# A hand-ordered attention and snake-MLP kernel: the steps of its first three blocks in another order

## The chip, the core and the metric

The kernel runs on one core of a Trainium2 chip. The metric is the time of one execution on the device in microseconds (us). It was measured three times before the change: 296.65 us is the median, 296.1 and 298.42 us are the lowest and highest. All rows of a profile come from one more execution, which the hardware profiler recorded.

## What is computed

For 8 batches, 8 heads, 576 positions and a head size of 64 the reference forms decayed causal attention without a softmax, lays the heads side by side, and sends the 4608 rows through a two-layer network of width 2048 whose activation is h + sin²(αh)/α:

```python
scores = scale * np.matmul(q, k.transpose(0, 1, 3, 2))
Dmat = np.where(rel >= 0, gamma[:, None, None] ** rel, 0.0)   # rel = row - column
x = np.matmul(scores * Dmat, v)          # heads side by side: (4608, 512)
h = x @ w_in                             # (512, 2048)
g = h + np.sin(alpha * h) ** 2 / (alpha + 1e-09)
out = g @ w_out                          # (2048, 512), float32
```

## The kernel before

**Blocks.** The first 512 positions of each batch make one block of 512 rows (blocks 0 to 7); the last 64 positions of all eight batches make block 8. For each block the attention gives x, transposed, as an fp16 tile xT; 16 projections of 128 channels follow (four products of 128x128 by 512 columns each), then sine, square and product for each channel group, and the second matrix product.

**Engines.** TensorE (PE) does all products. ScalarE (ACT) does every sine. VectorE (DVE) does every product step (square times 1/α plus h, read from PSUM), and the masks. Squares, casts of the loaded fp32 data to fp16, and evictions of PSUM go to ACT, DVE or GpSimd (POOL) as each step says. SyncE (SP) issues the loads of q, k and v, the transposing DMAs and the stores; POOL issues the eight loads of 512 KB of the weights.

**The steps, with their lines.** `load(b, nm, p)` (L147) brings half p of q, k or v of batch b into one of six buffers raw0 to raw5. `cast` (L171, the work in L207 or L122) makes fp16 of it. For batches 0 and 1 PE transposes (`turn`, L234, work in L240) and `take` (L247, work in L120 and L122) copies to kT or qT; from batch 2 on `crossed` (L226, L230) does it by a DMA. Within a batch `outer` (L312, L325) forms sums of k times v, `take_sum` and `evict` bring them to the tile kvs, `next_sum` (L352), `more` (L367, two instructions L370 and L371, on POOL) and `to_state` (L358; L361 on ACT, L363 elsewhere) chain them over the four chunks of 128 rows; `scores` (L379, L389), `masked` (L397, L401), `values` (L409, L430) and `add_states` (L441, L451) make the block's output and `keep` (L458) copies it to xT. `project` (L560, L568), `sine` (L573, L576), `square` (L581, L585 on ACT, L587 elsewhere) and `product` (L590, L592) work on one channel group; `gemm2(n, u)` (L600, L605) multiplies a quarter of the 2048 channels (part u mod 4) into the output rows of chunk u div 4; `finish` (L594) copies that bank to fp32 and stores it. `keep_busy(n, tag, m)` (L727, L730) issues n products of zeros of m columns; nothing reads them. `wait_for_w_in(g)` and `wait_for_w_out(g)` (L736, L740) are small DMAs from a weight tile, which hold SP's queue until that weight has landed.

**What sets the order.** L784 to L1263 are a list of these steps, written out, for blocks 0 to 2 (and what batches 3 and 4 need early). Each engine runs its instructions in the order of the list; between engines semaphores keep the dependencies. The number of the buffer that a step takes is read from the table BUFFERS (L19), in the order of the list; PSUM banks (h0, h1, h2, op of one bank, m0 and m1 of two) stand in the steps. From L1265 on a loop over n = 3 to 8 makes the order of the other blocks; there a block's second product is done in seven products of quarters (L671) in place of `gemm2` from n = 4 on.

The piece of the list that matters most for batch 1 (L937 to L970, with steps left out):

```python
        load(1, "v", 0)
        cast(1, "v", 0, G_)
...
        load(1, "k", 1)
        cast(1, "k", 1, G_)
...
        load(1, "v", 1)
        cast(1, "v", 1, A_)
...
        gemm2(0, 15, "h2")
        at[1].outer((1,), "h0", "h1")
        at[1].take_sum(2, A_)
```

Of the kernel before, what the change touches and what calls it, by code (L numbers as in the profile page):

```python
# [19 lines left out]
    "raw": "012345012345012345102405314023140240124012401240",  # L20
    "k16": "0123012302131313",
    "q16": "0120120121202020",
    "v16": "0123012310230123",
    "kT": "0123012310232323",
    "qT": "0123013210232323",
    "kvs": "00000000",
    "s16": "01010101",
    "xT": "01202020",
    "s32": "010101010101010101010",
    "ret": "01230123012313020213021302130213",  # L30
    "s": "012312013021302130210213021302130231032032103102320132013201320132013201320132013201320132013201320132013201320132013201320132013201320132013201",
    "ss": "012302130123012032103213021302103210321031203120312031203120312031203120312031203120312031203120312031203120312031203120312031203120312031203120",
# [4 lines left out]
def kernel(  # L37
# [74 lines left out]
    def load_w_out(g):  # L112
        nc.gpsimd.dma_start(w_out16[:, 4 * g : 4 * g + 4, :], w_out_r[:, g])
# [169 lines left out]
    class Attention:  # L283
# [268 lines left out]
    ops = {}  # L552
    PART = {None: slice(0, 512), 0: slice(0, 256), 1: slice(256, 512)}
# [46 lines left out]
    def gemm2(n, u, tag, cols=slice(0, 512)):  # L600
        c, part = divmod(u, 4)
        if (n, c, cols.start) not in ops:
            ops[n, c, cols.start] = psum.tile([P, 512], F32, tag=tag, bufs=1, name="ops")
        for fk in range(4 * part, 4 * part + 4):
            matmul(  # L605
                ops[n, c, cols.start][:, cols], gT[n][:, fk, c * P : (c + 1) * P], w_out16[:, fk, cols],
                start=(fk == 0), stop=(fk == FC - 1), skip_group_check=True,
# [173 lines left out]
    with tc.manual_schedule():  # L781
# [9 lines left out]

        keep_busy(7, "op", 128)
        keep_busy(6, "h0", 256)
        keep_busy(11, "op", 128)
        load(0, "k", 0)
        load(0, "q", 0)
        load(0, "v", 0)
        cast(0, "k", 0, V, (0,))
        cast(0, "k", 0, G_, (1,))
        turn(0, "k", 0, "op")  # L800
        cast(0, "q", 0, V, (1,))
        cast(0, "q", 0, V, (0,))
        turn(0, "q", 0, "h0")
        load(0, "k", 1)
        cast(0, "k", 1, G_, (0,))
        invert_alpha()
        cast(0, "v", 0, A_)
        at[0].outer((0,), "h1", "h2")
        keep_busy(8, "op", 256)
# [645 lines left out]
```

## Time and profile before

| what | value |
|---|---|
| median of three runs | 296.65 us (296.1 to 298.42) |
| the profiled execution | 298.54 us; its span from first to last instruction is 296.8 us |
| PE, DVE, ACT, POOL busy in the span | 284.6, 227.5, 207.3, 136.0 us |
| mean granted TensorE clock | 0.994 |
| first projection of block 0 starts | 21.16 us |
| projection 0 of block 3, the first step of the loop, done | 108.65 us |
| bytes moved by DMA | 50.08 MB, 169 GB/s |

Busy shares alone do not tell what a change can win: an engine that is busy 96% of the span may lose its other 4% in one place. So the profile is read by stages of the span, and in each stage by the wait that ends last. In a row of the timeline the columns are start, duration, engine, line, operation, tiles written and read, shape, count; square brackets give the idle time before it and what ended it. A row that joins several matmuls ends when the last one has drained: one of 512 columns is shown with 379 ns, but in the row of 24 of them from 77.98 us the starts are 216 ns apart ((5.35 - 0.379) / 23 us).

### The profile page before, as it was taken

The page shows a single profiled execution, that of the slowest core. Times are in us where ns is not written, and L with a number is a line of the kernel's source. Part 1 is how long each engine was busy: PE and PEld are TensorE (multiplying, and loading weights), DVE is VectorE, ACT ScalarE, POOL GpSimd, SP SyncE. Part 2 cuts the span into 40 slices and gives each one's busy share as a digit, 9 for nine tenths or more (in the row PEclk, how much of TensorE's full clock was granted, in tenths as well). Part 3 has the DMA queues.
Part 4 walks back from the last instruction along what each step waited for, and adds up shares of the span by engine and source line. Part 5 has one row for each costly group of instructions (what it writes and reads, how often), then busy time and mean ns, then how long its engine had stood idle before and what let it go on. Part 6 is the DMA issues. An engine that isn't in the chain of part 4 may idle for free. (4 is left out here: it accounts for less than half of the span.)

```text
span 296.8 us, 8464 instructions
## 1 busy us (share of the span) xinstructions
PE 284.6 (96%) x3480; PEld 183.6 (62%) x3480; DVE 227.5 (77%) x336; ACT 207.3 (70%) x341; POOL 136.0 (46%) x151
## 2 busy tenths in 40 slices
PE   6789997999999999999999999999999999999994
PEld 4666544555554554455767766776667676777783
DVE  2597873897628979778977598759876987987884
ACT  2579924798776796788866996698669657865510
POOL 5684676448299687652197219901970000000000
PEclk9999997999999999999999999999999999999999
DMA  7999999999899698967876897789962102111213
GB/s 218 347 232 210 247 255 286 281 257 242 220 204 218 102 185 175 270 162 143 156 200 202 147 189 183 220 145 157 222 163 58 40 10 81 35 38 35 71 33 111
DMA packets 122918, 50.08 MB, mean 169 GB/s; under 512 B 79872, under 2 KB 120832, under 8 KB 122880
## 3 DMA queue, kind: packets, MB, share of 16 engines
q1 hardware_dynamic: 118928, 44.78, 62.7%
q0 software_dynamic: 2688, 4.19, 7.8%
q10 hardware_dynamic: 1264, 0.58, 0.8%
q8 instruction: 27, 0.44, 0.6%
q14 instruction: 11, 0.09, 0.1%
HBM read 36.75 MB, written 9.44 MB: 156 GB/s over the span
## 5 line engine op out<-in xcount | busy, mean ns | idle before, releaser
L592 DVE SCALAR_TENSOR_TENSOR gT<-ss,inva,hps 128x512 f16<-128x512 f16 x144 | 105.4, 744 | 29.2 <-ACT ss L585 25.3
L576 ACT ACTIVATE s<-hps,alpha_t 128x512 f16<-128x512 f32 x144 | 96.8, 682 | 44.3 <-PE hps L568 43.9
L568 PE MATMUL hps<-xT,w_in 128*128 128x512 f16 (+1 forms) x532 | 121.3, 372 | 0.7 <-DMA w_in<-in_moe_w_in_dram 0.3
L568 PEld LDWEIGHTS <-w_in 128*128 128x128 f16 x596 | 66.6, 114 | 50.7 <-issue 1.4
L585 ACT ACTIVATE ss<-s 128x512 f16<-128x512 f16 x107 | 67.3, 630 | 2.8
L605 PE MATMUL ops<-w_out,gT 128*128 128x512 f16 x192 | 47.6, 385 | 0.0
L671 PEld LDWEIGHTS <-gT 128*128 128x128 f16 x384 | 37.5, 98 | 8.3
L207 POOL TENSOR_TENSOR k<-raw,cn 128x1024 f16<-128x1024 f32 (+1 forms) x17 | 28.9, 1703 | 7.5 <-DMA raw<-in_k_dram 7.5
L671 PEld LDWEIGHTS <-S 128*128 128x128 f16 x288 | 27.7, 98 | 5.3
L605 PEld LDWEIGHTS <-gT 128*128 128x128 f16 x192 | 18.1, 99 | 20.8 <-issue 0.6
L363 POOL TENSOR_TENSOR s<-kvs,cn 128x256 f16<-128x256 f32 x17 | 10.4, 612 | 41.8 <-DVE S L652 25.4
L207 POOL TENSOR_TENSOR q<-raw,cn 128x1024 f16<-128x1024 f32 x13 | 24.6, 1903 | 4.5 <-DMA raw<-in_q_dram 4.3
L671 PE MATMUL hps<-T,gT 128*128 128x256 f16 x192 | 22.9, 273 | 0.0
L671 PE MATMUL hps<-w_out,gT 128*128 128x256 f16 x192 | 22.9, 273 | 0.0
L671 PE MATMUL hps<-w_out,S 128*128 128x256 f16 x192 | 22.8, 273 | 0.0
L401 DVE TENSOR_TENSOR ret<-sc,mask 128x1024 f16<-128x1024 f32 x16 | 19.2, 1219 | 1.6 <-PE sc L389 1.4
L371 POOL TENSOR_TENSOR kvs<-s,kvs 128x256 f32<-128x256 f32 x21 | 16.0, 762 | 5.5 <-ACT kvs L120 2.8
L120 ACT CAST xT<-o 128x1024 f16<-128x1024 f32 (+1 forms) x15 | 16.5, 1129 | 2.7 <-PE o L451 2.7
L587 DVE TENSOR_TENSOR ss<-s 128x512 f16<-128x512 f16 x29 | 14.3, 495 | 3.0 <-ACT s L576 2.8
L370 POOL TENSOR_TENSOR s<-kvs,cn 128x256 f32<-128x256 f32 x21 | 13.3, 635 | 6.4 <-ACT kvs L120 6.3
L717 DVE TENSOR_TENSOR osb<-hps,low 128x512 f32<-128x512 f32 x13 | 9.0, 692 | 9.2 <-PE hps L671 9.2
L652 DVE TENSOR_TENSOR S<-gT,S 128x1024 f16<-128x1024 f16 x24 | 15.5, 685 | 0.0
(83 smaller groups left out, 274.6 us busy)
## 6 DMA issues: line engine op xcount, KB each, us to landing
raw<-in_q_dram SPq DMA_DIRECT2D x16, 512.0 KB, 5.4
out_dram<-osb SPq DMA_DIRECT2D x32, 256.0 KB, 2.8
raw<-in_k_dram SPq DMA_DIRECT2D x8, 512.0 KB, 6.1
raw<-in_v_dram SPq DMA_DIRECT2D x8, 512.0 KB, 5.3
raw<-in_v_dram SPq DMA_DIRECT2D x32, 128.0 KB, 3.4
raw<-in_k_dram SPq DMA_DIRECT2D x32, 128.0 KB, 3.2
w_in<-in_moe_w_in_dram POOLq DMA_DIRECT2D x4, 512.0 KB, 11.8
w_out<-in_moe_w_out_dram POOLq DMA_DIRECT2D x4, 512.0 KB, 13.1
```

The source lines that it names most:

```text
L120: eng.copy(d_, s_)
L207: eng.tensor_tensor(dst[:, a0:a1].rearrange("p a r t d -> p t (a r) d"), t_.rearrange("p (t a) x -> p t a x", t=2)[:, :, a0:a1].rearrange( ...
L371: nc.gpsimd.tensor_tensor(self.kvs[:, c], s32, self.kvs[:, c], ADD)
L401: nc.vector.tensor_tensor(ret.rearrange("p t (z x) -> p (t z) x", z=2)[:, :, 0:n], sc.rearrange("p t (z x) -> p (t z) x", z=2)[:, :, 0:n], ...
L568: matmul(hps_of[n, fc][0][:, cols], w_in16[fc // 4][:, a, fc % 4 :: 4], xs[n][:, a, cols], start=(a == 0 and part != 1), stop=(a == KT - 1 ...
L576: nc.scalar.activation(s_t, hps, mybir.ActivationFunctionType.Sin, bias=0.0, scale=alpha_t[:, fc : fc + 1],)
L585: nc.scalar.activation(ss_t, s_t, mybir.ActivationFunctionType.Square)
L587: eng.tensor_tensor(ss_t, s_t, s_t, MULT)
L592: nc.vector.scalar_tensor_tensor(gT[n][:, fc, :], ss_t, inva[:, fc : fc + 1], hps, MULT, ADD)
L605: matmul(ops[n, c, cols.start][:, cols], gT[n][:, fk, c * P : (c + 1) * P], w_out16[:, fk, cols], start=(fk == 0), stop=(fk == FC - 1), sk ...
L652: return eng.tensor_tensor(out_, x, y, op)
L671: matmul(acc[:, 256 * j : 256 * j + 256], lhs[:, x, 128 * j : 128 * j + 128], rhs[:, x], start=(tag is not None and j == js[0] and p == 0 ...
```

## The change

It leaves the loop from n = 3 on as it was and writes the list for blocks 0 to 2 anew: nearly every step stands elsewhere. The arithmetic is the same, with these differences:

- The tables of buffers are other ones for these blocks. In particular `load(1, "v", 1)` now takes raw2, the buffer of `load(1, "v", 0)`, where it had raw5 and the other raw3.
- Order of the first loads: q, k, v, q, k, v of batch 0 in place of k, q, v, k, q, v.
- Products of zeros: 50 in place of 36, all after the first transposes: 1 of 512 columns, 26 of 74, 20 of 128, then single ones; before, 24 of them stood ahead of the first real product.
- Steps on other engines: over the whole program squares on ACT, DVE and POOL are 97, 37 and 10 (before 107, 29 and 8); casts of v on ACT 12 (6), states on ACT 28 + 4 instructions (24); one `more` is on DVE; several casts and takes are halved between engines.
- Which of a chunk's four quarters comes first in `gemm2` is free: it is known from a list of the parts done.
- 14 instructions more run on PE, all of them zero products. The bytes moved and the waits for weight tiles are as many as before.

```diff
 BUFFERS = {
-    "raw": "012345012345012345102405314023140240124012401240",
+    "raw": "051243520202405124145312054231401240124012401240",
...
-        def more(self, c):
+        def more(self, c, eng=nc.gpsimd):
 
             s32 = place("s32", [P, 4, D], F32)
-            nc.gpsimd.tensor_tensor(s32, self.kvs[:, c - 1], g1.unsqueeze(2).to_broadcast([P, 4, D]), MULT)
-            nc.gpsimd.tensor_tensor(self.kvs[:, c], s32, self.kvs[:, c], ADD)
+            eng.tensor_tensor(s32, self.kvs[:, c - 1], g1.unsqueeze(2).to_broadcast([P, 4, D]), MULT)
+            eng.tensor_tensor(self.kvs[:, c], s32, self.kvs[:, c], ADD)
...
+        done = parts_of.setdefault((n, c), [])
+        done.append(part)
         for fk in range(4 * part, 4 * part + 4):
             matmul(
                 ops[n, c, cols.start][:, cols], gT[n][:, fk, c * P : (c + 1) * P], w_out16[:, fk, cols],
-                start=(fk == 0), stop=(fk == FC - 1), skip_group_check=True,
+                start=(len(done) == 1 and fk == 4 * part), stop=(len(done) == 4 and fk == 4 * part + 3),
+                skip_group_check=True,
             )
```

The new list at the start (`G_`, `V`, `A_` are POOL, DVE, ACT; steps of one engine after another are joined in a line):

```python
        load(0, "q", 0); load(0, "k", 0); load(0, "v", 0); load(0, "q", 1); load(0, "k", 1)
        cast(0, "k", 1, G_)
        cast(0, "q", 0, V, (0,)); cast(0, "q", 0, V, (1,))
        cast(0, "k", 0, V, (1,)); cast(0, "k", 0, V, (0,))
        turn(0, "q", 0, "h1"); keep_busy(1, "op"); turn(0, "k", 0, "h2"); keep_busy(26, "op", 74)
        cast(0, "q", 1, V)
        load(0, "v", 1); load(1, "q", 1); load(1, "q", 0); load(1, "k", 0)
        take(0, "q", 0, V); cast(0, "v", 0, A_); load_w_in(0)
        take(0, "k", 0, A_, (0,)); take(0, "k", 0, A_, (1,)); keep_busy(20, "h0", 128)
        turn(0, "q", 1, "op"); at[0].scores(0, 1, "m0")
        take(0, "q", 1, A_, (0,)); take(0, "q", 1, V, (1,))
        at[0].outer((0,), "op", "h0"); at[0].scores(0, 0, "m1"); at[0].take_sum(0, A_); load_w_in(1)
...
        at[0].values(1, False, "h1", "h0"); at[0].values(1, True)
        load_w_out(2); cast(1, "q", 0, G_, (1,)); load_w_in(3)
        at[0].to_state(1, A_); at[0].to_state(2, A_); at[0].keep(0, V, A_); at[0].take_sum(3, A_)
        at[0].add_states(1); take(1, "q", 1, A_); cast(1, "q", 0, V, (0,)); turn(1, "q", 0, "op")
        project(0, 1, "h2", 0); at[0].keep(1, V, A_); project(0, 1, "h2", 1)
```

Around the second half of batch 1:

```python
        load(1, "v", 0); cast(1, "v", 0, A_, (0,)); cast(1, "v", 0, A_, (1,)); load(1, "k", 1)
        sine(0, 15); product(0, 13); load(1, "v", 1); gemm2(0, 5, "op")
        cast(1, "k", 1, G_, (0,)); cast(1, "k", 1, V, (1,))
        gemm2(0, 13, "h2"); gemm2(0, 14, "h2"); at[1].outer((0,), "h0", "h1"); gemm2(0, 6, "op")
        turn(1, "k", 1, "h0"); gemm2(0, 12, "h2"); square(0, 15, V)
        at[1].masked(0, 1); at[1].values(0, False, "m0"); at[1].take_sum(1, A_); at[1].take_sum(0, A_)
...
        at[1].scores(1, 1, "m1"); at[1].values(0, True); gemm2(0, 15, "h2"); at[1].masked(1, 1)
        at[1].scores(1, 0, "m1"); at[1].more(1); cast(1, "v", 1, A_); at[1].masked(1, 0)
        at[1].outer((1,), "h0", "h1"); gemm2(0, 7, "op")
```

At the ends of blocks 1 and 2 (steps of PE left out where they play no part):

```python
        sine(1, 3); square(1, 4, A_); cast(3, "v", 0, A_); sine(1, 2); square(1, 3, A_); square(1, 2, A_)
...
        project(1, 15, "op"); at[3].outer((0, 1), "h2", "h1"); finish(0, 2, V)
        load(4, "v", 0); load(4, "k", 0); product(1, 4); product(1, 3); product(1, 2)
...
        at[3].evict_bank(0, V); square(1, 15, V); cast(3, "q", 1, V); product(1, 15); gemm2(1, 6, "h0")
...
        crossed(3, 1, "q"); crossed(3, 0, "q"); load(4, "q", 0)
...
        product(2, 1); load(4, "k", 1)
...
        cast(4, "k", 0, V); product(2, 7); at[3].more(3); square(2, 4, G_); cast(4, "v", 1, G_, (0,))
        cast(4, "k", 1, G_, (0,)); cast(4, "q", 0, G_); cast(4, "k", 1, V, (1,))
...
        finish(1, 2); sine(2, 3); product(2, 4); at[3].masked(0, 0)
```

More of the change, by code (lines that the diff above doesn't have):

```diff
@@ L1044 @@
[L1044 to L1054 removed]
+        project(1, 4, "h2")
+        gemm2(0, 11, "h0")
+        gemm2(0, 8, "h0")
+        gemm2(0, 10, "h0")
+        product(1, 9)
+        square(1, 13, V)
+        crossed(3, 1, "k")
@@ new lines @@
+        project(2, 6, "m0")
+        gemm2(1, 4, "h0")
+        project(2, 2, "h1")
+        project(2, 0, "op")
+        sine(2, 1)
+        sine(2, 6)
+        at[3].to_state(0, A_)
+        crossed(3, 1, "q")
+        crossed(3, 0, "q")
+        load(4, "q", 0)
+        sine(2, 2)
+        square(2, 1, G_)
+        at[3].more(1)
+        square(2, 6, V)
+        gemm2(1, 7, "h0")
+        project(2, 7, "m1")
+        project(2, 4, "h2")
+        at[3].scores(1, 1, "m0")
+        gemm2(1, 11, "h0")
```

771 lines of the change are left out of this document (380 added, 391 removed).

## The prediction

> **What bounds the kernel now.** I read the busy line first, then the time by stages, then PE's timeline around the one stage where PE falls short.
>
> ```profile
> PE 284.6 (96%) x3480; PEld 183.6 (62%) x3480; DVE 227.5 (77%) x336; ACT 207.3 (70%) x341; POOL 136.0 (46%) x151
> ```
> ```profile
> 0.00:13.50 13.50, 9.70 (x119) 7.41 (x120) 4.77 (x9) 4.63 (x6) 7.64 (x17) 1.00 0.95 276
> 13.50:21.20 7.70, 6.12 (x185) 4.25 (x184) 7.52 (x16) 6.53 (x12) 7.29 (x8) 1.00 1.20 254
> 21.20:43.60 22.40, 22.30 (x217) 13.24 (x218) 17.15 (x27) 15.76 (x26) 13.41 (x15) 1.00 1.10 238
> 43.60:52.00 8.40, 6.34 (x134) 3.41 (x133) 3.87 (x4) 3.65 (x9) 5.56 (x5) 0.80 0.94 276
> 52.00:107.80 55.80, 55.58 (x721) 29.65 (x720) 42.02 (x59) 44.51 (x77) 37.74 (x40) 1.00 0.93 216
> 107.80:200.00 92.20, 91.94 (x1148) 58.69 (x1147) 73.79 (x105) 73.61 (x120) 50.34 (x51) 1.00 0.81 182
> ```
>
> After the stage's length stand the busy times of PE, weight loads, DVE, ACT and POOL, then the granted clock, the DMA share and GB/s. PE is the bound from 21.2 us on: it lacks 0.10 us in the third stage, 0.22 in the fifth, 0.26 in the sixth. Only 43.6 to 52.0 is different: PE lacks 8.40 - 6.34 = 2.06 us and runs at a clock of 0.80, which costs another 0.20 x 8.40 = 1.68 us. PE's work is not changed, so after 21.2 us the new order has 2.06 + 1.68 + 0.10 + 0.22 = 4.06 us to win at most. Before 21.2 us PE is not the bound, and a chain of casts, copies and masks is.
>
> ```profile
> 21.16 8.97 PE L568 MATMUL hps<-xT,w_in 128*128 128x256 f16 x56 [0.33 <-DMA w_in<-in_moe_w_in_dram]
> 43.43 1.04 PE L605 MATMUL ops<-w_out,gT 128*128 128x512 f16 x4
> 46.43 0.45 PE L325 MATMUL kv<-v,k 64*64 64x64 f16 x32 [1.96 <-ACT v L120]
> 46.80 2.79 PE L605 MATMUL ops<-w_out,gT 128*128 128x512 f16 x8
> 77.98 5.35 PE L605 MATMUL ops<-w_out,gT 128*128 128x512 f16 x24
> ```
> ```profile
> 45.33 1.04 ACT L120 CAST v<-raw 128x1024 f16<-128x1024 f32 x1 [5.36 <-DMA raw<-in_v_dram]
> ```
> ```profile
> 0.80 0.46 SPq L158 DMA_DIRECT2D raw<-in_k_dram  x1
> ...
> 32.08 0.53 SPq L158 DMA_DIRECT2D raw<-in_v_dram  x1
> ...
> 33.51 2.91 SPq L158 DMA_DIRECT2D raw<-in_v_dram  x1
> ...
> 38.00 4.84 SPq L158 DMA_DIRECT2D raw<-in_k_dram  x1
> ...
> 84.56 2.65 SPq L230 DMA_TRANSPOSE qT<-q  x1
> ```
> ```profile
> 35.10 0.60 POOL L113 DMA_DIRECT2D w_out<-in_moe_w_out_dram  x1
> 37.98 1.03 POOL L122 CAST v<-raw 128x1024 f16<-128x1024 f32 x1 [2.29 <-DMA raw<-in_v_dram]
> 39.49 1.90 POOL L207 TENSOR_TENSOR k<-raw,cn 128x1024 f16<-128x1024 f32 x1 [0.47 <-DMA raw<-in_k_dram]
> ```
>
> The bad stage, read backwards: `outer` of batch 1's second half waited 1.96 us for a cast of v, the cast for a load. That load was issued at 33.51 and landed at 45.33, 11.8 us, while the two ahead of it were there at 37.98 and 39.49. The last w_out load (35.10) was issued next to it. After the gap PE needs 2.79 us for 8 products of 512 columns, where a row at full clock needs 0.216 us each (77.98: 24 in 5.35).
>
> **The change, part by part.** *The bad stage.* The new order puts the same seven quarters of `gemm2` ahead of that `outer`, but also `values` of the first half (0.75 us of PE: the 32 products from 18.01 below, less the drain of the last) and lets PE come later by the start's loss. The load of v now waits for its own buffer: v's first half must be cast from it. That cast moves to ACT in two halves, 37.95 + 1.1 = 39.05 us. The load then has no rival, since w_out has 4 us of DMA to itself.
>
> ```profile
> raw<-in_v_dram SPq DMA_DIRECT2D x8, 512.0 KB, 5.3
> raw<-in_k_dram SPq DMA_DIRECT2D x32, 128.0 KB, 3.2
> kT<-k SPq DMA_TRANSPOSE x12, 4.4
> ```
> ```profile
> 18.01 0.92 PE L430 MATMUL o<-ret,v 64*64 64x128 f16 x32
> 30.41 3.62 PE L568 MATMUL hps<-xT,w_in 128*128 128x512 f16 x16
> ```
>
> With the median of 5.3 us it lands at 44.35, with 4.1, as for the first load (issued at 0.80, used at 4.92), at 43.15; the cast of 1.04 ends at 44.2 to 45.4. PE arrives at 43.6 + 0.75 + 0.5 to 1 = 45 or so. So I take the wait as gone, and the low clock with it: +2.06 + 1.68. If the load takes the 11.8 us of before, `outer` starts at 39.05 + 11.8 + 1.1 = 51.95 us, 5.5 later than now; that end goes to a rival.
>
> *The start.* The weights cannot come earlier: w_in's first load ended PE's last wait before projections, and the loads ahead of it are the same nine.
>
> ```profile
> 9.61 2.04 POOL L207 TENSOR_TENSOR k<-raw,cn 128x512 f16<-128x512 f32 x2 [3.10 <-DMA raw<-in_k_dram]
> 11.59 2.43 POOL L110 DMA_DIRECT2D w_in<-in_moe_w_in_dram  x3
> ```
> ```profile
> 4.92 0.69 DVE L207 TENSOR_TENSOR k<-raw,cn 128x512 f16<-128x512 f32 x1 [3.69 <-DMA raw<-in_k_dram]
> 11.05 1.68 DVE L207 TENSOR_TENSOR q<-raw,cn 128x1024 f16<-128x1024 f32 x1 [2.81 <-DMA raw<-in_q_dram]
> 13.07 1.23 DVE L401 TENSOR_TENSOR ret<-sc,mask 128x1024 f16<-128x1024 f32 x1 [0.34 <-PE sc L389]
> 19.49 0.42 DVE L363 TENSOR_TENSOR s<-kvs,cn 128x256 f16<-128x256 f32 x1
> 19.86 1.34 DVE L122 CAST xT<-o 128x512 f16<-128x512 f32 x2
> 21.10 0.67 DVE L122 COPY qT<-tr 128x1024 f16<-128x1024 f16 x1
> ```
>
> Loads landed at 4.9 (issued at 0.8) and then each 1.5 us later (9.6, 11.05). DVE's chain from the first mask at 13.07 to the last copy of xT at 21.20 takes 8.13 us. The new chain has the same masks, sums and copies, plus half a copy of kT (0.34) and half a cast of q (0.69), less the state that ACT now takes (0.42 at 19.49): 8.7 us. It begins when q's second half, now the fourth load, is cast and q's first half copied: 9.6 + 1.68 + 0.67 = 11.95, then a scores step (0.42 us in the rows below): 12.45. End: 21.15, so nothing is lost, if PE has ended its zero products by 11.3.
>
> ```profile
> 1.29 3.38 PE L730 MATMUL idle<-zero 128*128 128x128 f16 x24 [1.29 <-DVE zero L790]
> 15.87 0.42 PE L389 MATMUL sc<-qT,kT 64*64 64x128 f16 x16
> ```
>
> Those 24 products of 18 x 128 + 6 x 256 = 3840 columns took 3.38 us, 1136 columns per us, where 30.41 shows 16 x 512 in 3.62, 2260 per us: at the start PE runs at half its speed, though the clock column says 1.00. The new zero products (26 x 74 + 20 x 128 = 4484 columns) start after k's transposes, about 8.7, and end at 8.7 + 4484/1136 = 12.65 at the slow rate, or 10.7 at the fast one. Slow, the chain loses 12.65 - 11.3 = 1.3 us. The old kernel has 7 + 6 + 11 of them done before 4.7 us, the new one has none, so it isn't plain that it is fast sooner. Between 0 and 1.5 I take 0.3, near the fast end, since PE now works without a gap from 7.9 us on.
>
> The Trainium skill (TensorE: Matmul & The Clock Gate, Part 1) says that a free-running window of about 3.4 us decides the clock, and that an idle window halves it. By this rule a gap of 1.96 us need not cost any clock; the trace shows 0.80 over 8.4 us after it, so the measurement decides. Were the rule's "idle window" taken at its word, only the 2.06 us would be there to win, and the sum below would give 298.54 - 2.06 + 1.3 = 297.8.
>
> *Block 1.* DVE's work in it: 16 products of 0.69 (2.06 / 3 at 70.88), 8 squares of 0.4, 4 masks of 1.2, and 5.7 us of copies, sums and a cast: 24.7 us. PE's: 16 projections and 7 quarters of 0.865, and 4 us of `outer`, `scores` and `values`: 24. In this stretch neither has room, so a late square shows. The tightest place is at the end: `project(1, 15)` needs the bank that `product(1, 3)` frees, and between `project(1, 3)` and it ACT does sine, square, cast of v, sine, square.
>
> ```profile
> 70.88 2.06 DVE L592 SCALAR_TENSOR_TENSOR gT<-ss,inva,hps 128x512 f16<-128x512 f16 x3 [1.49 <-ACT ss L585]
> ```
> ```profile
> 79.18 1.06 ACT L120 CAST v<-raw 128x1024 f16<-128x1024 f32 x1
> 85.96 1.27 ACT L576 ACTIVATE s<-hps,alpha_t 128x512 f16<-128x512 f32 x2
> 88.93 1.14 ACT L585 ACTIVATE ss<-s 128x512 f16<-128x512 f16 x2
> ```
>
> 2 x 0.63 + 2 x 0.57 + 1.06 + 0.69 for the product = 4.1 us. PE in that time does a projection (0.86), `values` and `add_states` of both halves (1.9: twice 0.75, and 0.4) and another projection (0.86): 3.6. Stall 0.5; `gemm2(1, 6)` behind it waits for `product(1, 12)`, some 0.2 more. I take 0.6; 0 if ACT runs ahead, 1.8 if v of batch 3, which lands about then, is late as well.
>
> *Block 2.* Let `cast(3, "q", 1, V)` end at c. SP then issues two transposing DMAs (2.65, and 1.4 as an estimate for the second, whose queue is awake), 512 KB of q (0.5) and four pieces of k (2.6); 3.2 us on, at c + 10.4, the last has landed. DVE is there at c + 9.7: it masks after the scores that PE reaches at c + 5.4 (the DMA's 4.4 lies under 5 us of PE's other work), then 1.2 for the mask, two products and a cast of k of 1.68. So DVE waits 0.7 us at `cast(4, "k", 1, V, (1,))`; behind it `product(2, 4)` is queued, and for its bank `gemm2(1, 1)` waits at c + 12.2: 10.4 + 0.7 + 0.7 = 11.8 would do. With the 4.4 us of other DMAs it is 0.8 late, and more comes behind, since DVE's masks follow. I take 0.4, of 0 to 1.6.
>
> *Nothing for* halved casts, other banks and buffers (they are in the chains above), `gemm2`'s free order, 14 zero products more (all before 21 us), and T3, POOL's states and the transposes for batch 4, which have 6 us until unit 3 of block 3. If those are late, PE's 0.26 us in the sixth stage grow.
>
> **Sum.** Against the profiled execution, 298.54: - 2.06 - 1.68 + 0.3 + 0.6 + 0.4 = - 2.44, so 296.1 us. The median of the runs is 296.65, 1.9 less than that execution, and one run of three is at 298.42: the low clock's 1.68 us may well be missing in the two lower runs. In the new kernel nothing should bring it, so 296.1 stands for the median too: no change that can be told, as about 1% (3 us) can.
>
> **The rivals.** *Faster by over 1%* (under 293.7): all of the order's stalls vanish and the low runs carry the low clock too, 296.65 - 4.06 = 292.6; or part of it. For it: over the whole fifth stage DVE and ACT have room (42.02 and 44.51 of 55.80 us), more than the tight places above let one think. Against it: the start can give nothing, and 298.54 - 4.06 = 294.5 is the floor if the profile is a typical execution of before. 0.15.
>
> *Slower by over 1%* (over 299.6): the load of v behind its own buffer. If it takes t us from 39.05, `outer` starts at 40.15 + t; up to t = 5 it costs nothing, at 11.8 it costs 5.5 + 1.68 against the forecast's none: 296.1 + 7.2 = 303.3. Over 299.6 it is from t = 8.5 on, with a low clock from 6.8. For it: this is how long it took before, and SP needed 4.84 us for an issue at 38.00; against it: w_out is out of its way. 0.17.
>
> *A slow PE at the start* alone adds 1.0 to the 0.3: 297.1, within 1%. *The low clock isn't tied to the gap* (1.68 less to win): 297.8, within 1%. *The change does nothing*, since PE arrives later and the wait only moves: 296.65.
>
> **How the numbers follow.** The forecast has 0.45, a slow start 0.1, no effect 0.08, the untied clock 0.05: 0.68 within 1%. Range: its low end is 293.6, the middle of the two floors (292.6 and 294.5); its high end, with the three losses at their upper ends, 298.54 - 3.74 + 1.5 + 1.8 + 1.6 = 299.7. Beyond these lie about 0.05 and 0.15.
>
> **What would show it.** Right: no wait of PE for ACT's v over 0.5 us, clock 1.00 from 21 to 107 us, block 3's first step some 2 us earlier, projections not before 21.1. Wrong: a gap at `outer` of batch 1, PE's zero products running past 11.3 us, waits of PE for product steps over 2 us in sum between 53 and 107.

## The result

| kernel | median | runs | ratio to before, 95% interval |
|---|---|---|---|
| before (beside the changed kernel) | 296.38 us | 4 (295.85 to 298.42) | 1 |
| changed | 310.36 us | 4 (308.52 to 311.19) | 1.045 (1.0377 to 1.0523) |

The change makes the kernel 14.0 us slower. An execution more than 1.5% above the fastest of its kernel is left out of the ratios and their intervals, here and below; the medians are of all. The forecast was 296.1 us, the range ended at 299.7. The profiled execution after took 309.6 us, its span is 307.9, against 298.54 and 296.8: 11.1 us of span to find.

The groups of ACT's sines show where. Counted from block 3 on, the i-th sine does the same work in both kernels; the difference of their starts is 7.26 us at the first sine of block 3 and 11.44 us at its fifth, and from its ninth on it stays at 11.10 to 11.18 us to the end. So all is lost before 135 us. (Against the second trace of the kernel before, shown below, the difference at the end is 14.07 us.) First the busy line and the stages of the changed kernel, in the columns known from before:

```profile
PE 287.7 (93%) x3494; PEld 182.8 (59%) x3494; DVE 239.9 (78%) x354; ACT 205.0 (67%) x344; POOL 127.6 (41%) x148
```
```profile
13.50:21.20 7.70, 5.24 (x191) 3.66 (x194) 6.92 (x14) 4.01 (x12) 6.09 (x9) 0.99 1.21 261
21.20:43.60 22.40, 21.77 (x196) 13.15 (x200) 17.82 (x32) 16.82 (x27) 13.27 (x15) 0.93 0.98 196
43.60:52.00 8.40, 8.28 (x180) 4.27 (x175) 5.79 (x7) 5.74 (x12) 5.66 (x6) 1.00 1.09 323
52.00:107.80 55.80, 52.29 (x681) 26.33 (x673) 43.64 (x61) 37.32 (x70) 31.49 (x34) 0.97 0.89 214
107.80:200.00 92.20, 89.75 (x1018) 55.01 (x1018) 75.39 (x104) 68.30 (x108) 48.15 (x53) 0.98 0.75 165
```

The stage that was bad (43.6 to 52.0) is good: PE lacks 0.12 us, the clock is 1.00. But PE now lacks 0.63 us from 21.2 to 43.6, 3.51 from 52.0 to 107.8 and 2.45 from there to 200, and in these three stages the clock is 0.93, 0.97 and 0.98. PE's timeline names the places (the brackets give the idle time and what ended it; rows in order, others left out):

```profile
22.39 1.01 PE L240 MATMUL tr<-ident,q 128*128 128x128 f16 x8 [0.18 <-ACT kvs L120]
23.30 1.01 PE L569 MATMUL hps<-xT,w_in 128*128 128x256 f16 x4
24.71 9.55 PE L569 MATMUL hps<-xT,w_in 128*128 128x256 f16 x56 [0.39 <-DVE xT L122]
...
48.42 0.42 PE L325 MATMUL kv<-v,k 64*64 64x64 f16 x32
...
54.62 3.19 PE L569 MATMUL hps<-xT,w_in 128*128 128x512 f16 x16 [0.63 <-ACT xT L120]
```
```profile
79.41 1.86 PE L569 MATMUL hps<-xT,w_in 128*128 128x512 f16 x4 [2.29 <-DVE gT L593]
...
116.39 1.02 PE L608 MATMUL ops<-w_out,gT 128*128 128x512 f16 x4 [0.29 <-DVE gT L593]
...
122.93 1.33 PE L569 MATMUL hps<-xT,w_in 128*128 128x512 f16 x4 [2.06 <-DVE gT L593]
124.19 0.85 PE L389 MATMUL sc<-qT,kT 64*64 64x128 f16 x32
124.98 1.89 PE L608 MATMUL ops<-w_out,gT 128*128 128x512 f16 x4
```

The first projection comes at 23.30 instead of 21.16. `outer` of batch 1 (48.42) has no wait. Two new gaps of 2 us, at 79.41 and 122.93, end with a product step. Each brought a period of 3.41 us at half clock (79.1 to 82.6 and 123.5 to 126.9): four products of 512 columns take 1.89 us at 124.98 where they take 1.03 at full clock. A third such period lies at 21.1 to 24.5.

**What the kernel before does in other executions.** It ran again with a profile; this is its second trace.

> The kernel before the change itself, for a second trace. If the gap of PE ahead of outer of batch 1 belongs to the order, it is there again (1.5 us or more, and sine 0 of block 1 at 54 to 55 us); if it was an event of the one profiled execution (a load of v that took 11.8 us), the gap is under 1 us and sine 0 of block 1 comes at 52 to 53 us. The time is 296.4 either way.

It took 295.56 us, with a median of 296.34 in 8 executions (ratio 1.0006, 0.9973 to 1.0040). Its stage from 43.6 to 52.0, and the rows there:

```profile
43.60:52.00 8.40, 8.19 (x148) 4.45 (x147) 7.11 (x9) 5.10 (x10) 7.38 (x6) 1.00 1.07 315
```
```profile
43.46 1.04 ACT L120 CAST v<-raw 128x1024 f16<-128x1024 f32 x1 [3.51 <-DMA raw<-in_v_dram]
```
```profile
44.56 0.45 PE L325 MATMUL kv<-v,k 64*64 64x64 f16 x32
...
50.43 1.89 PE L568 MATMUL hps<-xT,w_in 128*128 128x512 f16 x8
```

The same load, issued at the same time (33.49 us), was there for the cast at 43.46 instead of 45.33; `outer` starts without a wait; no period of low clock follows; block 1 starts at 50.43 instead of 53.50. So the wait of 1.96 us and the low clock, all the gain in the sum, belong to the one execution that was profiled, which took longer than any of the runs listed with it. The traces of two kernels that differ from the kernel before in the start alone (the probe and the one with fewer zero products, below) have no such wait either. Nor is a low clock what separates the times: of 49 executions of the kernel before that ran beside the experiments, the 25 with a mean clock under 0.99 have a median of 296.43 us and the 24 others 296.10; where in them the clock was low is not known.

One more kernel asks the same from the other side: the kernel before with more of PE's work ahead of that `outer`.

```diff
         gemm2(0, 15, "h2")
+        gemm2(0, 7, "op")
+        at[1].values(0, False, "m1")
+        at[1].values(0, True)
         at[1].outer((1,), "h0", "h1")
         at[1].take_sum(2, A_)
         at[1].more(2)
-        gemm2(0, 7, "op")
```

> Kernel before the change, one place: in batch 1 the quarter 7 of gemm2 and the values of the first half stand ahead of outer of the second half, 1.6 us of PE's work. Theory (the wait of 1.96 us for the late load and the low clock behind it are what that stage loses): the wait falls under 0.5 us, the clock stays at 1.00 from 21 us on, the time falls from 296.4 by 1.6 us in runs that had no low clock and by 3.3 in those that had, to 293 to 295. Rival (the stall only moves, since block 1 waits for its loads): the time stays at 296.4, with a new gap before 60 us.

Measured: 297.02 us, 1.0033 (1.0009 to 1.0056). In its profile the wait is gone (no interval over 0.8 us between two products there), yet the time did not fall: the rival's time, for a reason that neither text had. In this trace, too, the load was there early (the cast started at 43.57 us), so there was no wait to remove, and the run does not test what a late load would cost in this order.

### The profile page after: what moved, and what is told of

Its sections match the earlier page's. It is cut to its first block, busy times and chain, and to the rows that moved or that the text cites. A ratio compares the mean times of both kernels' runs of the same rounds, so it can differ in the third digit from the quotient of the medians.

```text
span 307.9 us, 8517 instructions
## 1 busy us (share of the span) xinstructions
PE 287.7 (93%) x3494; PEld 182.8 (59%) x3494; DVE 239.9 (78%) x354; ACT 205.0 (67%) x344; POOL 127.6 (41%) x148
## 5 line engine op out<-in xcount | busy, mean ns | idle before, releaser
L569 PE MATMUL hps<-xT,w_in 128*128 128x512 f16 (+1 forms) x532 | 124.2, 375 | 5.6 <-DVE gT L593 4.3
L586 ACT ACTIVATE ss<-s 128x512 f16<-128x512 f16 x97 | 61.0, 631 | 2.6 <-ACT s L577 0.2
L608 PE MATMUL ops<-w_out,gT 128*128 128x512 f16 x192 | 48.6, 386 | 0.3 <-DVE gT L593 0.3
L207 POOL TENSOR_TENSOR k<-raw,cn 128x1024 f16<-128x1024 f32 (+1 forms) x17 | 25.7, 1519 | 12.6 <-DMA raw<-in_k_dram 12.3
L207 POOL TENSOR_TENSOR q<-raw,cn 128x1024 f16<-128x1024 f32 (+1 forms) x14 | 24.0, 1718 | 9.1 <-DMA raw<-in_q_dram 7.4
L363 POOL TENSOR_TENSOR s<-kvs,cn 128x256 f16<-128x256 f32 x16 | 10.2, 640 | 42.2 <-DVE S L656 38.6
L588 DVE TENSOR_TENSOR ss<-s 128x512 f16<-128x512 f16 x37 | 22.4, 604 | 5.3 <-ACT s L577 4.8
L120 ACT CAST xT<-o 128x1024 f16<-128x1024 f32 (+1 forms) x15 | 17.2, 1164 | 5.7 <-DVE xT L122 3.8
L588 POOL TENSOR_TENSOR ss<-s 128x512 f16<-128x512 f16 x10 | 10.3, 1038 | 18.0 <-ACT s L577 18.0
L120 ACT CAST v<-raw 128x512 f16<-128x512 f32 (+1 forms) x12 | 9.3, 794 | 10.3 <-DMA raw<-in_v_dram 10.3
L371 POOL TENSOR_TENSOR kvs<-s,kvs 128x256 f32<-128x256 f32 x20 | 14.6, 729 | 2.5 <-DVE kvs L122 1.0
```

The source lines that it names most:

```text
L120: eng.copy(d_, s_)
L207: eng.tensor_tensor(dst[:, a0:a1].rearrange("p a r t d -> p t (a r) d"), t_.rearrange("p (t a) x -> p t a x", t=2)[:, :, a0:a1].rearrange( ...
L363: (eng or nc.gpsimd).tensor_tensor(self.state_of(c), self.kvs[:, c], g1.unsqueeze(2).to_broadcast([P, 4, D]), MULT)
L371: eng.tensor_tensor(self.kvs[:, c], s32, self.kvs[:, c], ADD)
L569: matmul(hps_of[n, fc][0][:, cols], w_in16[fc // 4][:, a, fc % 4 :: 4], xs[n][:, a, cols], start=(a == 0 and part != 1), stop=(a == KT - 1 ...
L586: nc.scalar.activation(ss_t, s_t, mybir.ActivationFunctionType.Square)
```

## The experiments

The theory after the result: the new order loses its time in four places of its own (the start, the end of block 1, the entry to block 3, and 0.6 us ahead of block 1), each through a dependency or a contention between two engines, and the low clock behind a gap makes each dearer. The rival: DVE and ACT are late throughout, so that a gap that is closed opens elsewhere.

### The end of block 1

```profile
76.42 1.05 ACT L120 CAST v<-raw 128x1024 f16<-128x1024 f32 x1 [1.78 <-DMA raw<-in_v_dram]
77.38 0.68 ACT L577 ACTIVATE s<-hps,alpha_t 128x512 f16<-128x512 f32 x1
77.96 1.14 ACT L586 ACTIVATE ss<-s 128x512 f16<-128x512 f16 x2
```
```profile
78.61 1.40 DVE L593 SCALAR_TENSOR_TENSOR gT<-ss,inva,hps 128x512 f16<-128x512 f16 x2 [2.89 <-ACT ss L586]
```

In the changed kernel ACT stands 1.78 us before the cast of v of batch 3 for its load, which is the last of six issued one after another from 61.80 us on. The squares of groups 3 and 2 are queued behind the cast, DVE's product behind them, and `project(1, 15)` behind that.

```diff
         square(1, 4, A_)
-        cast(3, "v", 0, A_)
         sine(1, 2)
         square(1, 3, A_)
         square(1, 2, A_)
+        cast(3, "v", 0, A_)
```

> Changed kernel, one place: ACT casts v of batch 3 (first half) behind the two squares of groups 3 and 2 of block 1, where it stood ahead of them. Theory (the squares were queued behind a cast that waits 1.78 us for its load, and PE lost 2.4 us to it and a low clock after it): the gap before project(1,15) falls from 2.50 us to about 0.5, the half clock at 79.1 to 82.6 is not granted, and the time falls by 2.0 + 1.6 = 3.6 us, to 306.8. Rival (ACT or DVE as a whole is late at the end of block 1): the gap moves to the sums of batch 3 behind it or to block 2, and the time falls by less than 1 us.

Measured: 306.79 us, 3.6 less than the changed kernel (ratio to before 1.0359, 1.0295 to 1.0423; the intervals touch, so the profile has to decide). In it the squares come first and PE does not wait:

```profile
75.58 1.15 ACT L586 ACTIVATE ss<-s 128x512 f16<-128x512 f16 x2
76.69 1.05 ACT L120 CAST v<-raw 128x1024 f16<-128x1024 f32 x1
```
```profile
77.45 1.05 PE L569 MATMUL hps<-xT,w_in 128*128 128x512 f16 x4
78.43 0.71 PE L325 MATMUL kv<-v,k 64*64 64x64 f16 x64
79.62 1.89 PE L608 MATMUL ops<-w_out,gT 128*128 128x512 f16 x8 [0.48 <-DVE gT L593]
```

`project(1, 15)` at 77.45 follows the products ahead of it at once, and no low clock comes once the start is over. What is left is 0.48 us at `gemm2(1, 6)`. The theory's 3.6 us came out in the median, but not as one place's gain. In this trace, of its fastest execution (304.55 us), the entry to block 3 is better too, though no step there was moved: PE's wait of 2.06 us is 0.52, with no low clock behind it.

```profile
121.78 1.02 PE L569 MATMUL hps<-xT,w_in 128*128 128x512 f16 x4 [0.52 <-DVE gT L593]
```

### The entry to block 3

Squares of DVE and what POOL does at the same time, in the changed kernel:

```profile
116.92 2.14 DVE L588 TENSOR_TENSOR ss<-s 128x512 f16<-128x512 f16 x1
...
120.42 1.68 DVE L588 TENSOR_TENSOR ss<-s 128x512 f16<-128x512 f16 x1
...
123.40 0.42 DVE L588 TENSOR_TENSOR ss<-s 128x512 f16<-128x512 f16 x1
```
```profile
116.88 1.90 POOL L207 TENSOR_TENSOR k<-raw,cn 128x1024 f16<-128x1024 f32 x1
118.72 1.23 POOL L122 CAST v<-raw 128x1024 f16<-128x1024 f32 x1
119.92 1.90 POOL L207 TENSOR_TENSOR k<-raw,cn 128x1024 f16<-128x1024 f32 x1
```

A square takes 0.42 us, but 2.14 and 1.68 beside POOL's casts. Of DVE's 37 squares in the whole trace 27 start while POOL is idle, with a median of 0.42 us, and 10 while it runs, with 0.99 us; the products, which read PSUM, take 0.74 us in both cases. The kernel before has 5 of 29 beside POOL, at 0.87 us. (Beside means that the POOL instruction ran on for at least 0.1 us.) Each of the ten in the changed kernel that met POOL ended 0.28 us after the POOL instruction beside which it had started, however long that one was: the square stood until then.

```diff
-        square(2, 15, V)
+        square(2, 15, A_)
```

> Changed kernel, one place: the square of group 15 of block 2 goes to ACT (it took DVE 2.14 us beside a cast on POOL). Theory (DVE's squares, which read and write SBUF alone, stand still while a POOL instruction runs; products, which read PSUM, do not): DVE gains 1.5 us or more there, the gap of 2.4 us at 120.5 shrinks under 1 us, the half clock behind it goes, and the time falls by 1.5 to 3.5 us, to 307 to 309. Rival (DVE merely has too many steps at block 3's start): DVE gains the 0.42 us of a square, the gap stays over 1.8 us, the time falls by less than 0.6 us.

Measured: 306.19 us, 4.2 less where 1.5 to 3.5 were expected (1.0302, 1.0240 to 1.0364, below the changed kernel's interval). The gap:

```profile
123.20 1.04 PE L608 MATMUL ops<-w_out,gT 128*128 128x512 f16 x4
124.41 1.02 PE L569 MATMUL hps<-xT,w_in 128*128 128x512 f16 x4 [0.18 <-DVE gT L593]
```

From 2.06 us it fell to 0.18, with no low clock behind it. The rival (DVE merely has too many steps) allowed 0.6 us. The contention by itself, ahead of the work of the kernel before:

```diff
+        probe = work.tile([P, 256], F16, tag="probe", bufs=1, name="probe")
+        nc.gpsimd.memset(probe, 0.0)
+        for _ in range(3):
+            nc.gpsimd.tensor_tensor(probe, probe, probe, MULT)
+        for _ in range(8):
+            nc.vector.tensor_tensor(zero, zero, zero, MULT)
```

> Kernel before the change with a probe ahead of its work: DVE multiplies a tile of zeros by itself 8 times (128x512 f16, in SBUF), POOL a 128x256 f16 tile of its own 3 times, from about 3 us on, with no wait between the two engines. Theory (DVE's instructions with both inputs in SBUF stand while a POOL instruction runs, and the other way round): the ones of DVE that run before POOL's first take 0.42 us, the ones that start beside POOL's last until that one ends, 0.6 us or more. Rival (they share nothing): 0.42 us for all eight. The probe computes nothing that the kernel needs.

The groups of these instructions (shortest, median, longest in ns) and the row of the cast behind them:

```profile
L796 DVE TENSOR_TENSOR zero<-zero x8: 424/424/715, 1.3 to 4.7; 128x512 f16<-128x512 f16 x8
```
```profile
L794 POOL TENSOR_TENSOR probe<-probe x3: 672/833/942, 4.3 to 5.9; 128x256 f16<-128x256 f16 x3
```
```profile
5.30 1.09 DVE L207 TENSOR_TENSOR k<-raw,cn 128x512 f16<-128x512 f32 x1
```

The eighth multiplication, which started at 4.66 us while POOL's first was running, took 715 ns, and the cast behind it 1.09 us instead of the 0.69 of the prediction's row. That multiplication ended 0.28 us after POOL's first, as the squares did. So the theory holds; with instructions as short as these the two engines take turns. By the Trainium skill (SBUF — State Buffer, SBUF: two separate sides) a DVE instruction with two inputs in SBUF and a GpSimd instruction that reads SBUF exclude each other for their whole length; trace and probe agree (0.42 against 0.99 us). The prediction did not use it.

### The start

These rows of DVE and ACT in the changed kernel stand in the start's chain. Those at 12.92 and 21.36 come ahead of the first projection's first half (23.30 us), the one at 23.93 ahead of its second half (24.71):

```profile
12.92 0.42 DVE L122 COPY qT<-tr 128x512 f16<-128x512 f16 x1 [1.57 <-ACT qT L120]
...
23.93 0.73 DVE L122 CAST xT<-o 128x512 f16<-128x512 f32 x1 [2.03 <-PE hps L569]
```
```profile
21.36 0.75 ACT L120 CAST xT<-o 128x512 f16<-128x512 f32 x1 [1.78 <-DVE xT L122]
```

In this trace steps that were halved between DVE and ACT run one after the other when both parts read one PSUM tile. PE's transposes of q ended at 12.26 us, ACT copied its part of qT from 12.30 to 12.88, and only then did DVE start on the other, 0.6 us late; ACT's part of xT's first half starts when DVE's has ended, 0.7 us late. (In the second half of xT the parts come from two PSUM tiles, and ACT's starts at 24.35, while DVE's runs until 24.66.) And DVE's part of xT's second half waits for products that read the first half: the instruction waits for them, presumably since what it writes and what they read overlap in the tile if each is taken from its first to its last address; the halves themselves do not overlap.

```diff
-        turn(1, "q", 0, "op")
-        project(0, 1, "h2", 0)
         at[0].keep(1, V, A_)
+        project(0, 1, "h2", 0)
         project(0, 1, "h2", 1)
+        turn(1, "q", 0, "op")
```

> Changed kernel, one place: the second half of xT of block 0 is kept before the first half's projection in the list, and the transposes of batch 1's q go behind the two halves of that projection. Theory (a dependency by the tile's range: the copy of the second half waits for the products that read the first): DVE's wait of 2.03 us before that copy falls under 0.5, PE's interval of 0.81 us between the two halves goes, projections run without a break from about 23.0 us, and sine 4 of block 0 starts 0.8 to 1.5 us earlier than 29.19; the time falls by about as much, to 309. Rival (DVE is late anyway): sine 4 at 29.0 to 29.2, time unchanged at 310.4.

Measured: 313.3 us (1.0538, 1.0452 to 1.0625), no gain, and in its trace sine 4 of block 0 comes 4.9 us later than before the edit, not earlier. DVE's wait of 2.03 us went as expected (0.35 us instead), but the first projection then waits 1.10 us for ACT's copy of batch 1's qT, which holds the bank h2. So ACT, not DVE, ends last there, which neither theory nor rival had. The clock in this trace is at half from 22.2 to 32.4 us, for three times as long as in the changed kernel's, so that what the edit alone is worth is not shown.

Zero products were the other suspect. One run takes them from the kernel before, one adds some to the changed kernel:

```diff
-        keep_busy(8, "op", 256)
...
-        keep_busy(3, "op")
...
-        keep_busy(1, "h1")
```

> Kernel before the change without its 12 products of zeros behind 9 us (8 of 256, 3 and 1 of 512 columns); nothing else is touched. Theory (these products keep the clock up through the start, where PE's real work has gaps): a clock of 0.5 for 3.4 us or more between 17 and 32 us, and 298 to 301 us. Rival (the clock does not depend on them, the low clock of the changed kernel's start is due to its later projections): 296, as before.

```diff
-        keep_busy(1, "op", 256)
+        keep_busy(3, "op")
...
+        keep_busy(2, "op")
         at[0].scores(1, 0, "m0")
```

> Changed kernel with 4 products of zeros of 512 columns more, in two gaps of PE between 14.9 and 16.6 us. Theory (the low clock of the start comes from PE's gaps there): a shorter low stretch or none at 17 to 32 us, 1.7 us or more off the 310.4 us. Rival (the gaps that count lie behind 18 us, where PE stands for code or DVE): the low clock stays, the time stays within 1 us.

Measured: 296.26 us (0.9989, 0.9966 to 1.0012) and 310.02 us (1.0462, 1.0400 to 1.0523), no difference in either. Without them the kernel before has its low clock from 7.5 to 14.3 us, when PE waits for casts anyway, and is at full clock from 14.3 on; with more of them the changed kernel still has 22.1 to 25.5 us at half. Both rivals were right: the missing zero products are not the cause.

### Mixed orders

Since the list alone sets the order, the old list up to a step can be followed by the new one's remaining steps, and the other way round, with the buffers chosen so that each is free.

> Mixed order, with buffers that fit it: the changed kernel's steps up to the first projection, then the old order. Theory (the start loses 2 to 3 us of chain, and PE's gaps there bring a low clock of one to three periods of 3.41 us, 1.7 to 5 us): first projection at 23 us or later, 299 to 303 us. Rival (the old order's slack at 44 us swallows the late start): 296 to 297.

> Mixed order, with buffers that fit it: the changed kernel's steps up to the first projection of block 2, then the old order. Theory (start, batch 1 and block 1 lose what they lose in the changed kernel, the entry to block 3 does not): 304 to 307, so that block 2 and the entry to block 3 are worth 3 to 6 of the 14 us. Rival (block 2 costs nothing by itself, and the gap at block 3 comes from what stands ahead): 309 to 311.

> Mixed order: the old steps up to the first projection, the load of batch 1's k issued behind the other first loads with its old buffer, then the changed kernel's order. (The two earlier mixes of this kind made one load of batch 1 wait for its buffer and PE stood 4.8 and 6.4 us for it.) Theory (the new start alone is worth the 6.4 us that its own mix lost): 310.4 - 6.4 = 304 us, within 1.5, first projection by 21.5 us and no low clock before 70 us. Rival (the rest of the new order rests on its own start): over 307.

Measured: 302.36 us (1.0225, 1.0180 to 1.0270) with the new start alone; 305.18 us (1.0317, 1.0261 to 1.0372) with new order up to block 2; 307.5 us (1.0368, 1.0311 to 1.0424) with the old start and the new rest. By the second, block 2 and the entry to block 3 are worth 310.36 - 305.18 = 5.2 us, 4.2 of which the one square gave back. By the third, the start is worth 310.36 - 307.5 = 2.9 us ahead of the new rest; the theory had expected 6.4 there. Its interval overlaps the changed kernel's, but the traces agree: with the old start the sines of block 0 come 2.5 to 3.2 us earlier. The 6.4 us of the first mix hold more than that: in its trace the clock is at half from 19.4 to 33.1 us, and it has a fault of its own. It calculates 1/α ahead of xT's second half, and this instruction of 16 columns stood for 3.35 us, until POOL's row of casts and issues ended at 26.94:

```profile
23.63 3.35 DVE L737 TENSOR_SCALAR inva<-alpha_t 128x16 f32<-128x16 f32 x1
```
```profile
25.01 1.93 POOL L207 TENSOR_TENSOR k<-raw,cn 128x1024 f16<-128x1024 f32 x1
```

Five other mixes have buffers that do not fit their order, and their times are not used.

> Mixed order: the changed kernel's steps up to the first projection, then the old order for all that is left. Theory (the start alone loses 2 to 3 us of chain and, as PE runs with gaps from 13 to 24 us, a stretch of low clock behind it): the first projection at 23 us or later, a granted clock of 0.5 for one to three periods of 3.41 us between 19 and 32 us, 299 to 301 us. Rival (the old order's wait for the late load at 44 us swallows a late start): 296 to 297.

> Mixed order: the changed kernel's steps up to the first projection of block 1, then the old order. Theory (between the start and block 1 the new order loses only the 0.8 us for the serial halves of xT, but no longer waits for v of batch 1): within 1 us of the kernel with the new start alone, 299 to 302. Rival (batch 1 in the new order makes everything behind it late): over 303.

> Mixed order: the changed kernel's steps up to the first projection of block 2, then the old order. Theory (block 1 loses 2.0 us at project(1,15) and 1.6 to the low clock behind it, and some 0.5 in small waits): 3 to 4 us over the mix that changes at block 1, 303 to 305; the remaining 5 to 7 us to the changed kernel's 310.4 are block 2 and the entry to block 3, where DVE's squares stand behind POOL. Rival (block 2 itself costs under 3 us): over 307.

> Mixed order: the old steps up to the first projection, then the changed kernel's order for all that is left. Theory (the new start costs 2 to 3 us and 1.7 to 5 us of low clock, and the rest of the losses stand): 303 to 306, clock 1.00 from 13 us to the gap at project(1,15). Rival (the start's loss is swallowed later by other waits): 309 to 311.

> Mixed order, with buffers that fit it: the old steps up to the first projection, then the changed kernel's order. Theory (the start's loss and its low clock go, the rest stands): first projection at 21 to 21.5 us, clock 1.00 from there to the gap at project(1,15), 303 to 306 us. Rival (the new order behind the start gives the same time whatever the start): 309 to 311.

In the first three, k of batch 1 was loaded into the buffer of batch 0's v ahead of that v's cast, so that part of the sums is of other data and the cast waited for the later load (304.6, 310.51 and 314.83 us). In the other two (315.61 and 315.9 us) one load of batch 1 waited for the cast that frees its buffer, its place ahead of the weights' loads was lost, and PE stood 4.76 and 6.42 us for it: in the last one k of batch 1 was issued at 15.95 us instead of 11.13, 4.8 us later, and its cast came at 30.26 instead of 21.87, 8.4 us later.

### Together

The three edits that concern stalls of their own (cast, square, and `gemm2(0, 1, "h0")` put ahead of `project(1, 8, "m1")`), first alone, then with the old start:

> Changed kernel with three edits together: the cast of v of batch 3 behind the two squares, the square of group 15 of block 2 on ACT, and the quarter 1 of gemm2 of block 0 ahead of block 1's first projection. Theory (these are stalls of their own, 3.6, 4.2 and 0.7 us, of which the first two overlap by the 1 to 2 us that the gap at block 3 already shrank with the first edit alone): 302 to 304. Rival (each edit alone has taken what all can give): 306.

> As the mix with the old start and the new rest, and with the three edits (the cast of v behind the squares, the square of group 15 on ACT, the quarter of gemm2 ahead of block 1). Theory (the losses are local and add up): 304.2 - 6.4 = 297.8 us, within 1.5; if the remaining order is better than the old one, under 295. Rival (some loss is in every stage and goes with no single edit): over 300.

Measured: 304.22 us (1.0274, 1.0241 to 1.0306) and 302.91 us (1.0218, 1.0166 to 1.0270). The first is close to the theory's 302 to 304. The second is not: 297.8 was expected, and over 300 was the rival's. The gains of 3.6, 4.2 and 2.9 us, 10.7 in sum, are 7.5 together. Its profile by stage, and the waits that are left:

```profile
43.60:52.00 8.40, 7.54 (x143) 3.75 (x144) 7.21 (x10) 4.48 (x9) 5.06 (x4) 1.00 0.98 289
52.00:107.80 55.80, 51.81 (x658) 26.13 (x657) 45.08 (x59) 37.58 (x72) 33.40 (x37) 1.00 0.89 211
```
```profile
71.64 1.89 PE L569 MATMUL hps<-xT,w_in 128*128 128x512 f16 x8 [1.77 <-DVE gT L593]
...
118.64 1.02 PE L569 MATMUL hps<-xT,w_in 128*128 128x512 f16 x4 [0.99 <-DVE gT L593]
```
```profile
69.00 0.62 ACT L120 CAST v<-raw 128x512 f16<-128x512 f32 x1 [2.39 <-DMA raw<-in_v_dram]
```

With the clock at 1.00 PE still lacks 0.86 and 3.99 us in these stages; in the second trace of the kernel before it lacks 0.21 and 0.87. Other product steps now come late; the wait at 71.64 has again a cast of v ahead of a square on ACT, which stood 2.39 us for its load (0.46 in the changed kernel). The sines show where each kernel gains. The table gives how many us earlier than in the changed kernel's trace a sine starts:

| sine | cast moved | square moved | old start and three edits |
|---|---|---|---|
| 5th of block 1 | -0.56 | -2.46 | 2.95 |
| 13th of block 1 | -0.47 | -2.40 | 0.74 |
| 5th of block 2 | 2.75 | -1.09 | 3.58 |
| 2nd of block 3 | 1.92 | -1.59 | 2.62 |
| 6th of block 3 | 5.02 | 2.38 | 5.85 |

The end of block 1 (second row to third) gives 3.2 us to the kernel with the cast moved and 2.8 to the one with all edits. The entry to block 3 (fourth row to fifth) gives 4.0 us for the square, but also 3.1 for the cast alone, and 3.2 for all edits. So the gains of the two edits overlap there, and their sum counts that place more than once; in the last column new waits also take back 2.2 and 1.0 us between the places. The -2.46 of the second column goes with a low clock of 10.2 us at the start of that one execution. So theory and rival share it: local stalls hold about half of the 14 us, and the rest moves on when they are closed. No kernel that was run beats the kernel before by more than its interval.

## Why the prediction was wrong, step by step

The miss is 310.36 - 296.1 = 14.3 us. The gain that was not there accounts for 1.6 of it, since the execution that it was read from was itself 298.54 - 296.38 = 2.16 us over the median: 3.74 - 2.16. The other 12.7 us are the losses, put at 0.3 + 0.6 + 0.4 = 1.3 and measured at 14.0. That is the step that failed most: the start was put at 0.3 and cost 2.9, the end of block 1 at 0.6 and cost 3.2, the entry to block 3 at nothing and cost 3 to 4, in part because a low clock behind a gap was put at nothing.

- **The gain, - 2.06 - 1.68.** This step comes first in the sum and failed, though it is the smaller part. The sum took the profiled execution's wait and low clock for the order's, though the text noted that this execution was 1.9 us over the median and that the low clock "may well be missing in the two lower runs". The second trace has neither. In it PE lacks 22.40 - 22.31 = 0.09, then 0.21 and 0.87 us in the three stages from 21.2 to 107.8: about 1.2 us to win, not 4, from a time of 295.56.
- **The stage itself was read rightly.** `load(1, "v", 1)` was issued at 41.84 us (39.05 expected; ACT's cast of the first half ended that much later), took 3.8 us, and `outer` had no wait. The rival on the slower side, this load behind its own buffer, did not happen. The result is on its side by another mechanism.
- **The start, + 0.3.** The zero products ended at 11.82 us, between the two bounds (10.7 and 12.65), and the first mask came at 13.26 for an expected 12.45. But the sum ended at DVE's chain. What it left out: parts of one PSUM tile are read one after the other (0.6 us at qT, 0.7 at xT), the bank of the first projection is freed by ACT's last copies, and the second half of xT waits for the first half's products. It also left out a pause of PE, 0.71 us long at 18.95 us (see the last section), behind which DVE's mask at 19.47 waited 0.40 us for its scores. Its bounds were 0 to 1.5; measured 2.9 us.
- **Block 1, + 0.6.** The place and the mechanism were right, named down to the five steps of ACT, and so was the upper end, "if v of batch 3, which lands about then, is late as well". It was late: 2.29 us of PE. The mis-sized term is 0.6; with the low clock, which the sum had at nothing ("in the new kernel nothing should bring it"), the place was worth 3.2 us in the traces, and the cast 3.6 in the median, part of it at the entry to block 3.
- **Block 2, + 0.4.** DVE waited 0.86 us for the load of batch 4's k where 0.7 was expected, and PE's timeline shows no wait from 82 to 116 us. The step was right, and cost PE nothing. That a second transposing DMA is issued faster than the first (1.52 us behind 2.65 in the trace before) is seen; the reason given for it was not tested.
- **Nothing for the entry to block 3.** The prediction gave T3, the states and the transposes 6 us of cover and asked only whether they were late. It did not put DVE's and POOL's instructions beside each other. Squares on DVE rose from 29 to 37, and 10 of them met POOL. This was worth 4.2 us by the square's own edit. How much is lost there hangs on the moment: in the trace with the cast moved only one of two squares stood (2.12 us), the other took 0.41 us beside a cast of POOL that took 2.21 in place of 1.90, and PE waited only 0.52.
- **Halved casts and copies at nothing.** What the halved casts from SBUF cost was not measured. For copies from PSUM it was wrong: the 0.63 us ahead of block 1 (54.62) are the two halves of xT in turn, too.
- **Two slips of the text.** 11.95 and a scores step of 0.42 make 12.37, not 12.45; and by the rival's own rule (free up to 5 us) a load of 11.8 us would cost 6.8 us, not 5.5. Neither changes the outcome.

Terms as the runs give them, place by place: 2.9 us for the start, 3.2 for the end of block 1, 3.1 to 4.0 for the entry to block 3, 0.6 ahead of block 1. That leaves 3 to 4 of the 14 us, which is a difference and not a measurement. Small waits could hold it, and so could the changes between products of 512 columns and short ones, of which the new order has 23 in place of 14 from the first projection to block 3; these were not separated.

## What to carry to other kernels

Before a stall in a profile is counted as something to win, look whether it is in a second execution; a load's landing can move by 2 us from run to run. Where an order is judged by hand, walk not only each engine's queue but the pairs: what DVE and GpSimd run at the same time, which halves share a PSUM tile, and which wait stands ahead of unrelated work in an in-order queue. And price a new gap of PE with the clock that may follow it. Before the gains of single edits are added up, look in each trace for the place where the gain arose.

## What the runs showed of the hardware

A gap of PE of about 2 us is followed by a low clock in some executions and not in others. In all the profiles together there are 15 intervals of 2.07 to 3.34 us between the starts of two products, later than 40 us; with 8 of them the clock was 0.5 for 3.4 or 6.8 us, with 7 it stayed at 1.00, among them one of 2.44 us, while others of 2.44 us were followed by it. This fits the Trainium skill (TensorE: Matmul & The Clock Gate, Part 1), by which the window is free-running, so that its phase decides; that the window has to be idle as a whole does not fit, since 2.34 us sufficed in the trace before.

A low clock costs nothing while PE is not the bound: the kernel before without its late zero products was at half clock from 7.5 to 14.3 us and took as long as with them.

In the changed start PE stands idle for 0.44 to 1.32 us near 18 to 20 us, in the middle of a row of `values`, with no wait for a semaphore in the profile. Eight traces with that start have it. In each of them a packet of 16 KB on the queue that the profile calls "instruction" ends 1.27 to 1.39 us before PE goes on, while the time of that end itself varies from 17.56 to 18.94 us. This fits a PE that waits for its code; no run moved that packet, so the cause is not shown.
